# A planned order searched again, with eleven durations changed and one weight sum moved from TensorE to VectorE

## The chip, the core and the metric

The kernel runs on one core of a Trainium2 chip. The metric is the device time of one execution in microseconds (us). Before the change it is 673.11 us, the median of three runs (671.66 to 673.67). The engines are named as the profile names them: PE is TensorE's matmul and PEld its weight load, DVE is VectorE, ACT is ScalarE, POOL is GpSimd, SP is the engine that issues most DMAs.

## What is computed

An attention block with a state that is updated token by token, and then a gated feed-forward network:

```
k_n = k / (norm(k) + 1e-6)
for t in range(S):
    y[:, :, t] = einsum('bhd,bhde->bhe', q[:, :, t], state)
    v_old = einsum('bhde,bhd->bhe', state, k_n[:, :, t])
    state += beta_t * einsum('bhd,bhe->bhde', k_n[:, :, t], v_t - v_old)
x = y as (tokens, heads * 48);  xn = x / sqrt(mean(x * x) + 1e-6) * rms_g
out = (silu(xn @ w_gate) * (xn @ w_val)) @ w_out
```

There are 4 batches, 8 heads, 768 tokens and 48 elements per head, so x has 3072 rows of 384. The weights w_gate and w_val are 384 x 1536 and w_out is 1536 x 384. Weights come as 64-bit floats and are brought to 32 bits on the chip; all products are in float32.

## The kernel before

**Stages.** The tokens are cut into twelve chunks of 64 tokens for all batches and heads (c = 0 to 11). Within a chunk the recurrence is solved as a triangular system: products of k with k (`scores`, L704), an inverse built by columns on VectorE (`prep16` for c = 0 and 1, `invert` for the others, L1070 and L1076), then products with the state (L1199, L1210), with the inverse (L1281) and with q (L1317), and the new state (L1404). The result goes through the root mean square (L1445 the square on ScalarE, L1452 and L1455 the sum and the power on GpSimd, L1465 the scaling, L1475 or L1495 the product with rms_g) into the tile xf. Chunks 0 and 1 take the feed-forward part as plain products (`ffn_plain`, L1558 up and L1540 down). From chunk 2 on `ffn` makes 30 block products per chunk out of sums of weight blocks (L1651, with the sums on VectorE, L1661), and `down` seven more (L1708).

**Weights.** `weights(n0, n1)` brings 18 tiles of 128 x 768. Each is loaded as pairs of 32-bit words. ScalarE makes one part of the float from the upper word (L619), VectorE makes another from both (L607, L610, L615), and the two are added. For tile n < NPE the addition is made on TensorE, as two products with the identity into one PSUM bank (L631, L632), and ScalarE copies the bank to w_in (L636). For the other tiles one VectorE instruction adds them (L639). NPE is 1, so only tile 0 goes over TensorE; it is split in two, one of 512 and one of 256 columns.

**What sets the order.** The program has no order of its own: `P.add(engine, duration, function, priority, reads, writes, ...)` only records an operation with its duration in us, and `Plan.run` (L303) decides in what order each engine gets them. Every DMA on SP's queue is such an operation too. `forward` plays the operations through on five engines and picks, at each step, the one that could start first. It counts TensorE's instructions and lets them come in blocks of 256 (L27 and L28, `supply`): a block is asked for at one place of the block before it and lacked at a later one, and a late block lengthens the operation. Where TensorE stood still for more than 1.4 us before an operation starts, from 70 us on, 1.6 us are added for a slow clock. `backward` gives new keys from the end, `shake` moves the keys at random from a number of the list MOVES. `run` goes through the rounds and then the moves, and keeps the order with the smallest reckoned end. Until 70 us, where TensorE has nothing to do, products with the identity (L1826) are put in between to keep it running.

ScalarE's durations are written as A(n) = 0.2 + 0.0008 n, VectorE's as V(n) = 0.13 + 0.0011 n. The planner lets two neighbours of ScalarE overlap by 0.1 us.

**Lines that the change touches:** L26 ROUNDS and MOVES; L403 NPE; in `setup`, L511 the identity on GpSimd, L534 `places2` on VectorE, L535 the warm-up activation; in `weights`, L619; in `invert`, L1039 `start` (its copy is L1028) and L1040 `start2` (its copies are L1034); in `recur`, L1445, L1457 `root` (L1452 to L1455), L1465, L1475 and L1495.

## Time and profile before

| | us |
|---|---|
| median of three runs | 673.11 (671.66 to 673.67) |
| the profiled execution, its own time | 677.52 |
| its span, first to last instruction | 675.8 |
| TensorE matmul busy in the span | 657.2 |
| TensorE weight load busy | 607.2 |
| VectorE busy | 576.2 |
| ScalarE busy | 297.9 |
| GpSimd busy | 88.0 |

The profile is one execution. A line such as L1651 is a line of the kernel; where an operation is written in a helper or in a function that is handed to `P.add`, the line is that of the instruction in the function. In a list of groups, the columns after the bar are the time that the group is busy, the mean of one instruction in ns, and how long the engine stood idle just before such instructions, with what ended the wait. "issue" as a cause means that the engine waited for nothing that the profile shows. The granted clock is that of TensorE, as a share of its full speed; over the whole span it is 0.995.

### The profile page before, as it was taken

To read this page: it belongs to the slowest core of one execution; us is meant where nothing else is said; L and a number is where in the kernel's file an instruction comes from. 1 tells how busy PE (TensorE), PEld (TensorE's weight loads), DVE (VectorE), ACT (ScalarE), POOL (GpSimd) and SP (SyncE) were. 2 spreads that over 40 slices of the span, in tenths; PEclk is the share of its full clock that TensorE was granted. 3 is DMA by queue.
4 is the path that set the end of the run, shared out by engine and by line. 5 is a ranking of instruction groups with operands and counts; after the bars stand their busy time and mean duration, and the time that the engine had idled before them with its cause. 6 is when DMAs were issued, how large, how long until landed. Compare 5 with 4: busy or idle time off the path is not lost.

```text
span 675.8 us, 23477 instructions
## 1 busy us (share of the span) xinstructions
PE 657.2 (97%) x10052; PEld 607.2 (90%) x10052; DVE 576.2 (85%) x1200; ACT 297.9 (44%) x683; POOL 88.0 (13%) x105
## 2 busy tenths in 40 slices
PE   8898999999999999999899999999999999999997
PEld 6876777778799999999899999999999999999997
DVE  5998889999999998997899899899899699457473
ACT  7553543524336445345246336246345344343341
POOL 4113111031031030030030021030031001000000
PEclk9998999999999999999899999999999999999999
DMA  9574577636415457347447437457437434202100
GB/s 227 127 191 129 118 191 165 137 59 112 63 24 96 68 132 117 59 110 116 74 101 126 77 90 132 82 117 123 80 77 125 80 58 82 47 2 48 24 1 24
DMA packets 270430, 64.40 MB, mean 95 GB/s; under 512 B 256979, under 2 KB 262134, under 8 KB 270326
## 3 DMA queue, kind: packets, MB, share of 16 engines
q1 hardware_dynamic: 267046, 62.12, 46.5%
q8 instruction: 79, 1.29, 0.8%
q10 hardware_dynamic: 3280, 0.79, 0.6%
q14 instruction: 25, 0.20, 0.1%
HBM read 45.30 MB, written 17.56 MB: 93 GB/s over the span
## 4 chain that ended last, share of the span: by engine, by line
PE 65%; DVE 21%; SPq 5%; DMA 4%; issue 3%; ACT 1%; POOL 0%; DVEq 0%; POOLq 0%; ACTq 0%
PE bank L1651 35%; PE bank L1708 15%; SPq L487 5%; DVE acc L1076 4%; DVE acc L1070 3%; PE bank L1558 3%; PE bank L704 3%; PE bank L1199 2%; PE bank L1317 1%; DVE tmp L1661 1%; DMA at<-dkk 1%; PE bank L1540 1%; DVE more L1616 1%; DMA q<-in_q_dram 1%; DMA x2bd<-dx 1%
## 5 line engine op out<-in xcount | busy, mean ns | idle before, releaser
L1651 PE MATMUL bank<-xf,w_in 128*128 128x128 f32 x1440 | 179.2, 276 | 0.6 <-DVE tmp L1661 0.6
L1651 PEld LDWEIGHTS bank<-xf,w_in 128*128 128x128 f32 x1440 | 169.8, 192 | 1.7 <-DVE tmp L1661 0.8
L1661 DVE TENSOR_TENSOR tmp<-tmp,bank 128x512 f32<-128x512 f32 x180 | 119.8, 680 | 27.9 <-PE bank L1651 24.3
L1651 PE MATMUL bank<-xf,more 128*128 128x128 f32 x960 | 124.9, 277 | 1.8 <-DVE tmp L1661 1.8
L1651 PEld LDWEIGHTS bank<-xf,more 128*128 128x128 f32 x960 | 115.2, 192 | 4.3 <-DVE tmp L1661 3.2
L1663 ACT COPY tmp<-bank 128x512 f32<-128x512 f32 x120 | 68.1, 585 | 64.8 <-PE bank L1651 52.9
L1667 ACT ACTIVATE tmp<-tmp 128x256 f32<-128x256 f32 x120 | 49.7, 417 | 98.0 <-DVE tmp L1661 97.3
L731 POOL TENSOR_TENSOR knrm<-ksum,half 128x16 f32<-128x16 f32 x12 | 35.8, 2981 | 324.8 <-DVE ksum L730 309.5
L1076 DVE TENSOR_REDUCE acc<-acc 128x30 f32<-128x90 f32 (+4 forms) x150 | 70.9, 473 | 5.1
L1708 PE MATMUL bank<-wo_sb,hf 128*128 128x192 f32 x360 | 64.0, 328 | 0.0
L1708 PEld LDWEIGHTS bank<-wo_sb,hf 128*128 128x128 f32 x360 | 58.2, 191 | 0.7 <-ACT tmp L1713 0.2
L1070 DVE TENSOR_TENSOR acc<-acc,at 128x60 f32<-128x60 f32 (+4 forms) x150 | 52.7, 351 | 2.3
L1668 DVE TENSOR_TENSOR hf<-tmp 128x256 f32<-128x256 f32 x120 | 48.5, 420 | 6.6 <-ACT tmp L1667 5.5
L1540 PE MATMUL bank<-wo_sb,hf 128*128 128x384 f32 x96 | 35.3, 496 | 1.9 <-DVE hf L1566 1.8
L1558 PE MATMUL bank<-xf,w_in 128*128 128x256 f32 x144 | 34.8, 392 | 0.2 <-DVE hf L1566 0.2
L1558 PE MATMUL bank<-xp,w_in 128*128 128x256 f32 x144 | 33.8, 382 | 0.0
L1558 PEld LDWEIGHTS bank<-xp,w_in 128*128 128x128 f32 x144 | 26.8, 190 | 5.5 <-DVE hf L1566 0.3
L1558 PEld LDWEIGHTS bank<-xf,w_in 128*128 128x128 f32 x144 | 26.9, 192 | 4.7 <-DVE hf L1566 0.5
L1565 ACT ACTIVATE tmp<-bank 128x256 f32<-128x256 f32 x24 | 9.2, 383 | 43.7 <-PE bank L1558 36.4
L1713 ACT COPY tmp<-bank 128x192 f32<-128x192 f32 x30 | 9.5, 317 | 42.0 <-PE bank L1708 40.2
L1540 PEld LDWEIGHTS bank<-wo_sb,hf 128*128 128x128 f32 x96 | 17.3, 190 | 11.8 <-DVE hf L1566 3.7
L1510 DVE TENSOR_TENSOR xf<-xf 128x256 f32<-128x256 f32 (+1 forms) x70 | 24.0, 382 | 1.9 <-ACT xf L1475 1.1
(203 smaller groups left out, 988.6 us busy)
## 6 DMA issues: line engine op xcount, KB each, us to landing
at<-dkk SPq DMA_DIRECT2D x20, 256.0 KB, 3.8
more<-in_moe_w_gate_dram SPq DMA_DIRECT2D x6, 768.0 KB, 5.3
vt<-in_v_dram SPq DMA_DIRECT2D x24, 192.0 KB, 4.2
k<-in_k_dram SPq DMA_DIRECT2D x23, 192.0 KB, 4.3
out_dram<-tmp SPq DMA_DIRECT2D x46, 96.0 KB, 2.2
more<-in_moe_w_val_dram SPq DMA_DIRECT2D x5, 768.0 KB, 7.0
more<-in_moe_w_out_dram SPq DMA_DIRECT2D x5, 768.0 KB, 7.3
dsq<-k SPq DMA_DIRECT2D x6, 512.0 KB, 2.6
```

The source lines that it names most:

```text
L487: op = P.add(eng, dur + (0.08 if eng == "SP" else 0.0), lambda: queue.dma_start(out=dst, in_=src), prio, r, w, lat=0.7)
L731: P.add("POOL", 2.95, lambda: nc.gpsimd.tensor_tensor(out=knrm[i2], in0=ksum[i2], in1=half, op=ALU.pow), pn, r=[("ksum", i2), "half"], w=[ ...
L1070: nc.vector.tensor_tensor(out=acc[:, 1:3, 0:n, j + 2 : W].rearrange("p a i t -> p i a t"), in0=acc[:, old, 0:n, j : j + 2, None].to_broadc ...
L1076: nc.vector.tensor_reduce(out=acc[:, new, 0:n, j + 2 : W], in_=acc[:, lo : lo + 3, 0:n, j + 2 : W].rearrange("p a i t -> p i t a"), axis=A ...
L1540: nc.tensor.matmul(po[p].t[:, 0:DM], hf[:, spot(f), 128 * p : 128 * p + 128], wo_sb[:, spot(f)], start=(f == f0), stop=(f == f1 - 1), skip ...
L1558: nc.tensor.matmul(ps.t[:, TOK * side : TOK * side + TOK], w_in[:, side, h_, 3 * t + i_, n : n + 128], x_[:, 2 * t : 2 * t + 2].rearrange( ...
L1651: nc.tensor.matmul(g.t[:, 128 * z : 128 * z + 128], fac[:, side, 128 * f : 128 * f + 128], xf[:, xs], start=(begin and z == 0), stop=False ...
L1661: P.add("DVE", V(512), lambda t=t, g=g: nc.vector.tensor_tensor(out=t, in0=t, in1=g.t, op=ALU.add), -1, r=[g], w=[tk], last=g)
L1663: P.add("ACT", A(512), lambda t=t, g=g: nc.scalar.copy(t, g.t), -1, r=[g], w=[tk], last=g)
L1667: P.add("ACT", A(256), lambda t=t: nc.scalar.activation(out=t[:, 0:256], in_=t[:, 0:256], func=ACTF.Silu), -1, w=[tk])
L1668: P.add("DVE", V(256), lambda t=t, f0=f0, p=p: nc.vector.tensor_tensor(out=hf[:, spot(f0) : spot(f0) + 2, 128 * p : 128 * p + 128], in0=t[ ...
L1708: nc.tensor.matmul(g.t[:, 0:192], a_[:, f], b_[:, f], start=(begin and f == 0), stop=(f == 5), skip_group_check=True)
```

## The change

Three things are changed. The seeds and the numbers of moves of the search are others: 24 as seed and 20 rounds with 585 moves, where it was 22, 17 rounds and 278 moves. NPE goes from 1 to 0, so the sum of weight tile 0 is made on VectorE by the same instruction as for the other 17. And eleven durations that the planner reckons with are others. No instruction is changed otherwise, but the order of the instructions on every engine, and of the DMAs in their queues, comes out of the search anew.

```diff
-ROUNDS, MOVES = (22, 17), (22002180, 22002182, 22003335,
...
+ROUNDS, MOVES = (24, 20), (24000254, 24000519, 24001431,
...
-    NPE, NRAW, NCV = 1, 3, 2
+    NPE, NRAW, NCV = 0, 3, 2
...
-        P.add("POOL", 1.0, lambda: make_identity(nc, ident), 0, w=["ident"])
+        P.add("POOL", 0.6, lambda: make_identity(nc, ident), 0, w=["ident"])
...
-        P.add("DVE", 0.9, places2, 2, r=["ident"], w=["put"])
-        P.add("ACT", 1.7, lambda: nc.scalar.activation(out=rs[0], in_=mhalf, func=ACTF.Silu), -1, r=["half"], w=[("rs", 0)])
+        P.add("DVE", 1.32, places2, 2, r=["ident"], w=["put"])
+        P.add("ACT", 0.25, lambda: nc.scalar.activation(out=rs[0], in_=mhalf, func=ACTF.Silu), -1, r=["half"], w=[("rs", 0)])
...
-            P.add("ACT", 0.84, lambda high=high, top=top: nc.scalar.activation(
+            P.add("ACT", 0.92, lambda high=high, top=top: nc.scalar.activation(
...
-        P.add("ACT", 0.5, start, pd, r=["half"], w=AK)
-        P.add("ACT", 0.9, start2, pd + 0.5, r=bkeys, w=AK)
+        P.add("ACT", 1.05, start, pd, r=["half"], w=AK)
+        P.add("ACT", 0.66, start2, pd + 0.5, r=bkeys, w=AK)
...
-                    P.add("ACT", A(384) + 0.2, lambda p=p, gy=gy: nc.scalar.activation(
+                    P.add("ACT", A(384), lambda p=p, gy=gy: nc.scalar.activation(
...
-            P.add("POOL", 1.1 if c else 0.7, root, py, r=["half"],
+            P.add("POOL", 1.1, root, py, r=["half"],
...
-                    P.add("ACT", A(384), lambda p=p: nc.scalar.mul(yn[:, p], yn[:, p], rs[i2][:, p : p + 1]),
+                    P.add("ACT", A(384) + 0.1, lambda p=p: nc.scalar.mul(yn[:, p], yn[:, p], rs[i2][:, p : p + 1]),
...
-                    P.add("ACT", A(256), lambda k_=k_: nc.scalar.mul(xf[:, 2 * k_ : 2 * k_ + 2],
+                    P.add("ACT", A(256) + 0.09, lambda k_=k_: nc.scalar.mul(xf[:, 2 * k_ : 2 * k_ + 2],
...
-                    P.add("ACT", A(128), lambda p=p, psx=psx, k_=k_: nc.scalar.mul(
+                    P.add("ACT", A(128) + 0.07, lambda p=p, psx=psx, k_=k_: nc.scalar.mul(
```

More of the change, by code (lines that the diff above doesn't have):

```diff
@@ L25 @@
 OVERLAP = {"PE": 0.0, "ACT": 0.1, "DVE": 0.08, "POOL": 0.06, "SP": 0.0}
-ROUNDS, MOVES = (22, 17), (22002180, 22002182, 22003335, 22003342, 22003359, 22003366, 22003748, 22003755, 22003872, 22003889, 22003903, 22003920, 22003934, 22003951, 22003980, 22004653, 22004660, 22004729, 22004746, 22004753, 22004770, 22004784, 22004801, 22004870, 22004877, 22004894, 22004901, 22004918, 22004925, 22004932, 22004949, 22004994, 22005011, 22005221, 22008697, 22008780, 22010194, 22010220, 22010239, 22010256, 22010270, 22010287, 22010301, 22010318, 22010400, 22010466, 22010535, 22010559, 22010560, 22010566, 22010583, 22010590, 22010614, 22010676, 22010683, 22010700, 22010707, 22010714, 22010731, 22010738, 22013940, 22014280, 22014565, 22014620, 22014780, 22014860, 22015546, 22015640, 22016400, 22016640, 22019860, 22020512, 22020620, 22020980, 22021900, 22022178, 22022500, 22023240, 22023744, 22024759, 22025599, 22028580, 22432695, 22434395, 22436663, 22437300, 22438400, 22439440, 22441380, 22441780, 22442460, 22442900, 22730144, 22731520, 22731920, 22731968, 22731982, 22732667, 22734384, 22734484, 22734852, 22735265, 22735300, 22735678, 22736628, 22736790, 22736838, 22737523, 22737533, 22737829, 22738662, 22738951, 22740560, 22746034, 22747420, 22747741, 22748419, 22749152, 22749290, 22753826, 22754194, 22755471, 22755620, 22756220, 22756789, 22757140, 22758049, 22758160, 22759790, 22760680, 22762300, 22763820, 22766102, 22766200, 22767004, 22767644, 22767940, 22768119, 22769086, 22771213, 22773629, 22773808, 22776028, 22785537, 22851960, 22853134, 22856837, 22860912, 22861215, 22862065, 22863655, 22864481, 22865240, 22865320, 22866860, 22869820, 22898160, 22899809, 22901540, 22901620, 22902120, 22902927, 22906589, 22906700, 22907300, 22907540, 22908258, 22910819, 22910877, 22911445, 22912860, 22913386, 22918927, 22919082, 22919880, 22920476, 22922892, 22922909, 22923180, 22923960, 22924706, 22926702, 22926967, 22928120, 22928416, 22928557, 22929276, 22929700, 22938627, 22940028, 22940145, 22940630, 22942998, 22943731, 22944000, 22944137, 22944285, 22944574, 22944715, 22945414, 22946570, 22947417, 22947699, 22948384, 22948477, 22950700, 22951100, 22952944, 22955921, 22956334, 22957415, 22967671, 22968620, 23135508, 23135773, 23136045, 23136069, 23136100, 23136186, 23137876, 23138585, 23139731, 23139865, 23140612, 23140877, 23142006, 23142520, 23143245, 23144220, 23144460, 23144640, 23145389, 23146680, 23149200, 23149620, 23149700, 23149932, 23151911, 23153000, 23153329, 23155077, 23155490, 23157118, 23160928, 23161513, 23163940, 23166040, 23172120, 23180693, 23181278, 23181371, 23181691, 23181722, 23182283, 23182383, 23182407, 23182782, 23182803, 23183216, 23183388, 23183512, 23183653, 23183694, 23183949, 23184090, 23184107, 23186217, 23186499, 23186967, 23187091, 23188237, 23188502, 23191307, 23191751, 23194752, 23194814, 23196170, 23233009)
@@ new lines @@
+ROUNDS, MOVES = (24, 20), (24000254, 24000519, 24001431, 24001703, 24001720, 24001796, 24001813, 24001844, 24002412, 24002429, 24002436, 24002505, 24002529, 24002620, 24002646, 24002825, 24003699, 24004205, 24179060, 24179074, 24179098, 24179105, 24179112, 24179129, 24179140, 24179198, 24179215, 24179222, 24179277, 24179322, 24179339, 24179340, 24179353, 24179363, 24179370, 24179377, 24179401, 24179425, 24179494, 24179511, 24179525, 24179532, 24179542, 24179611, 24179618, 24179635, 24179649, 24179659, 24597779, 24597780, 24597810, 24597827, 24597903, 24597917, 24598364, 24598371, 24598395, 24598440, 24598457, 24598460, 24598471, 24598481, 24598488, 24598502, 24598620, 24598700, 24601260, 24601293, 24601307, 24601310, 24601324, 24601331, 24601334, 24601338, 24601341, 24601348, 24601355, 24601372, 24601417, 24601434, 24601441, 24601455, 24601458, 24601472, 24601482, 24601489, 24601500, 24601513, 24601520, 24601565, 24601582, 24601589, 24601600, 24601603, 24601606, 24601620, 24601630, 24601637, 24601661, 24601706, 24601723, 24601730, 24601737, 24601744, 24601751, 24601754, 24601785, 24601792, 24601861, 24601871, 24601878, 24601885, 24601895, 24601902, 24601920, 24601940, 24602002, 24602009, 24602016, 24602019, 24602026, 24602033, 24602040, 24602043, 24602050, 24602057, 24602064, 24602074, 24603280, 24603289, 24603568, 24603575, 24606056, 24606080, 24609002, 24609009, 24631655, 24631662, 24631703, 24631748, 24645394, 24645400, 24684840, 24690920, 24701668, 24701675, 24701833, 24701840, 24701909, 24701919, 24701926, 24701933, 24701940, 24701943, 24701957, 24701974, 24702050, 24702057, 24702067, 24702074, 24702098, 24702105, 24702174, 24702191, 24702205, 24702208, 24702222, 24702229, 24702236, 24702239, 24702253, 24702270, 24702340, 24702463, 24702480, 24702494, 24702501, 24702511, 24702518, 24702587, 24702600, 24702604, 24702611, 24702621, 24702628, 24702635, 24702649, 24702652, 24702659, 24702666, 24702673, 24702683, 24702690, 24702759, 24702769, 24702790, 24703805, 24704366, 24704373, 24704390, 24704442, 24704459, 24704466, 24704480, 24704483, 24704490, 24704507, 24704514, 24704520, 24704521, 24704538, 24704583, 24704590, 24704600, 24704607, 24704621, 24704628, 24704631, 24704638, 24704652, 24704655, 24704686, 24704731, 24704738, 24732520, 24732522, 24751692, 24751778, 24817117, 24817124, 24817138, 24817145, 24817148, 24817155, 24817162, 24817172, 24817179, 24817248, 24817255, 24817265, 24817272, 24817279, 24817286, 24817293, 24817296, 24817303, 24817320, 24817372, 24817389, 24817396, 24817403, 24817410, 24817413, 24817420, 24817427, 24817434, 24817437, 24817444, 24817585, 24817592, 24817616, 24817661, 24817668, 24817678, 24817692, 24817699, 24817709, 24817716, 24817733, 24817747, 24817764, 24817800, 24817809, 24817816, 24817833, 24817840, 24817847, 24817850, 24817854, 24817880, 24817888, 24817957, 24817964, 24817971, 24817974, 24817981, 24817995, 24817998, 24818005, 24818019, 24818029, 24818036, 24818081, 24818098, 24818105, 24818112, 24818115, 24818119, 24818122, 24818129, 24818143, 24818146, 24818160, 24818177, 24818246, 24818253, 24818260, 24818263, 24821006, 24822097, 24849680, 24849682, 24858637, 24869300, 24875980, 24881500, 24883780, 24885640, 24885880, 24885891, 24886607, 24888727, 24889540, 24890280, 24891040, 24892117, 24892420, 24892936, 24893848, 24894082, 24894526, 24896140, 24900780, 24901158, 24901430, 24902460, 24902841, 24902896, 24903464, 24903640, 24904321, 24904555, 24905467, 24905553, 24905732, 24906606, 24907280, 24909920, 24911562, 24911834, 24912860, 24912918, 24914515, 24916222, 24917929, 24918160, 24918208, 24920049, 24921054, 24921326, 24921500, 24923305, 24923570, 24927125, 24927156, 24929493, 24934440, 24942024, 24942857, 24944688, 24951180, 24951780, 24952077, 24952094, 24952607, 24953137, 24956052, 24956180, 24956699, 24957540, 24958000, 24958131, 24958609, 24959721, 24959817, 24959848, 24960399, 24962815, 24963245, 24965124, 24966222, 24966511, 24967623, 24967960, 24968490, 24969213, 24969330, 24970290, 24970476, 24970906, 24970980, 24972479, 24977115, 24982501, 24983093, 24985220, 24987044, 24987488, 24989680, 24989725, 24991322, 24994416, 25013985, 25018490, 25019223, 25019643, 25025122, 25026733, 25030257, 25030446, 25030800, 25030976, 25032115, 25032931, 25215798, 25216211, 25216507, 25216748, 25217302, 25308605, 25309440, 25310164, 25310422, 25310873, 25311286, 25312301, 25312480, 25315237, 25318255, 25318899, 25319064, 25319081, 25319346, 25323655, 25324220, 25332100, 25333700, 25336820, 25339540, 25339700, 25339745, 25340175, 25342894, 25347740, 25348445, 25349020, 25353240, 25355440, 25360047, 25362587, 25362980, 25363571, 25365247, 25376180, 25382445, 25400159, 25401640, 25505975, 25506147, 25506450, 25506856, 25507152, 25507689, 25692363, 25692487, 25692494, 25692520, 25692597, 25692728, 25693189, 25693306, 25777354, 25777360, 25777791, 25777932, 25861550, 25862121, 25862658, 25862806, 25862923, 25863226, 25864100, 25864348, 25864379, 25864785, 25866072, 25866516, 25867366, 25867779, 25869039, 25869056, 25869338, 25869486, 25869634, 25869782, 25869868, 25869930, 25871286, 25871754, 25871954, 25873427, 25873840, 25874855, 25874955, 25875547, 25875564, 25875736, 25876032, 25878534, 25878565, 25878713, 25878830, 25879126, 25879398, 25879508, 25879959, 25880675, 25881105, 25881549, 25881649, 25881797, 25881931, 25881962, 25882258, 25882616, 25883180, 25883239, 25883786, 26020539, 26020556, 26020773, 26021895, 26022370, 26023953, 26024187, 26024201, 26024507, 26026214, 26026937, 26027219, 26027367, 26027584, 26027632, 26029043, 26029752, 26030280, 26030764, 26031177, 26032736, 26032853, 26033982, 26034278, 26034443, 26034839, 26035689, 26035780, 26035837, 26036298, 26036422, 26037220, 26037513, 26038660, 26039072, 26041880, 26043660, 26044740, 26046200, 26047460, 26047986, 26050260, 26050581, 26051228, 26053040, 26057079, 26057600)
@@ L615, in s5 @@
                 nc.vector.scalar_tensor_tensor(out=cc, in0=low, scalar=by, in1=cc, op0=ALU.mult, op1=ALU.mult)
-            P.add("ACT", 0.84, lambda high=high, top=top: nc.scalar.activation(out=top, in_=high.bitcast(FP32), func=ACTF.Prelu, scale=2.0**-112, alpha=2.0**32), pr, r=rk, w=cak)
+            P.add("ACT", 0.92, lambda high=high, top=top: nc.scalar.activation(out=top, in_=high.bitcast(FP32), func=ACTF.Prelu, scale=2.0**-112, alpha=2.0**32), pr, r=rk, w=cak)
             P.add("DVE", 0.57, s2, pr, w=cak)
@@ L1455, in root @@
                 nc.gpsimd.tensor_tensor(out=rs[i2][:, cols], in0=ms[i2][:, cols, 0], in1=mhalf[:, cols], op=ALU.pow)
-            P.add("POOL", 1.1 if c else 0.7, root, py, r=["half"], w=[(k_, i2, p) for p in h for k_ in ("ms", "rs")])
+            P.add("POOL", 1.1, root, py, r=["half"], w=[(k_, i2, p) for p in h for k_ in ("ms", "rs")])
             if c == 0:
@@ L1464, in recur @@
                 for p in range(2):
-                    P.add("ACT", A(384), lambda p=p: nc.scalar.mul(yn[:, p], yn[:, p], rs[i2][:, p : p + 1]), py, r=[("rs", i2, p)], w=[("yn", p)])
+                    P.add("ACT", A(384) + 0.1, lambda p=p: nc.scalar.mul(yn[:, p], yn[:, p], rs[i2][:, p : p + 1]), py, r=[("rs", i2, p)], w=[("yn", p)])
             if c >= XSQ:
@@ L1474, in recur @@
                 for k_ in range(KT):
-                    P.add("ACT", A(256), lambda k_=k_: nc.scalar.mul(xf[:, 2 * k_ : 2 * k_ + 2], xf[:, 2 * k_ : 2 * k_ + 2], g_sb[:, k_ : k_ + 1]), pxv, r=["g"], w=[xkeys[0]] + ([xkeys[1]] if k_ == KT - 1 else []))
+                    P.add("ACT", A(256) + 0.09, lambda k_=k_: nc.scalar.mul(xf[:, 2 * k_ : 2 * k_ + 2], xf[:, 2 * k_ : 2 * k_ + 2], g_sb[:, k_ : k_ + 1]), pxv, r=["g"], w=[xkeys[0]] + ([xkeys[1]] if k_ == KT - 1 else []))
                 continue
```

## The prediction, on record before the result

> **What bounds the kernel.** I read the head of the page first, then the busy time by stretch, then TensorE's waits, then the order of time around the two longest of them.

> ```profile
> span 675.8 us, 23477 instructions
> ...
> PE 657.2 (97%) x10052; PEld 607.2 (90%) x10052; DVE 576.2 (85%) x1200; ACT 297.9 (44%) x683; POOL 88.0 (13%) x105
> ...
> q8 instruction: 79, 1.29, 0.8%
> ```

> TensorE (PE) is busy 97% of the span, ScalarE (ACT) 44%, GpSimd (POOL) 13%. The last line is the queue that brings instructions. TensorE has 10052 matmul and 10052 weight-load records, and 20104 over 79 is 254: so I read q8 as TensorE's own supply, one packet of 16 KB for each 256 or so of its instructions. The next lines are the busy time of TensorE (matmul, then weight load), VectorE, ScalarE and GpSimd, the granted clock and the DMA share in four stretches:

> ```profile
> 0.00:41.00 41.00, 36.21 (x816) 29.60 (x817) 32.67 (x95) 26.59 (x52) 12.22 (x23) 1.00 0.79 189
> 41.00:190.00 149.00, 143.52 (x2080) 113.57 (x2078) 138.77 (x271) 61.16 (x134) 23.83 (x19) 0.99 0.56 122
> 190.00:640.00 450.00, 445.54 (x6912) 432.40 (x6913) 386.21 (x802) 200.80 (x477) 51.93 (x64) 1.00 0.46 85
> ```

> The first product of the feed-forward part (L1558) starts at 41.02 us. Of the 36.21 us before it, 8.93 are the warming products of L1826, so that stretch is a chain of dependences. From 41 us TensorE is idle 5.5 us of 149, then 4.5 of 450. So the end is: the start of L1558, plus TensorE's own work, which a new order doesn't shorten, plus TensorE's stalls. The longest of these, from 41 us on (us in total, times, longest):

> ```profile
> PE bank L704 <- issue: 3.0, 1, 3.0
> PE bank L1651 <- DVE tmp L1661: 2.4, 6, 0.8
> PE bank L1540 <- DVE hf L1566: 1.8, 3, 0.7
> PE bank L1199 <- issue: 1.5, 1, 1.5
> PE bank L1152 <- ACT tmp L1713: 0.5, 1, 0.5
> ```

> "issue" means that no engine or transfer released the product. The order of time shows both such stalls inside runs of small products, and the windows after them show the clock (column before the DMA share):

> ```profile
> 50.28 0.99 PE L704 MATMUL bank<-qt,kt 64*64 64x64 f32 x54
> 54.28 0.34 PE L704 MATMUL bank<-qt,kt 64*64 64x64 f32 x8 [3.02 <-issue]
> ```

> ```profile
> 328.47 0.87 PE L1199 MATMUL bank<-state,qt 48*64 48x48 f32 x47
> 330.88 0.49 PE L1199 MATMUL bank<-state,qt 48*64 48x48 f32 x17 [1.54 <-issue]
> ```

> ```profile
> 55.15:58.56 3.41, 3.41 (x69) 2.58 (x67) 0.91 (x2) 0.50 (x4) 1.62 (x1) 0.50 0.51 129
> 331.63:335.04 3.41, 3.41 (x13) 3.41 (x12) 1.18 (x4) 0.64 (x2) 0.00 (x0) 0.50 0.18 26
> ```

> The one block of 64 L704 products stands still after 56, the one of L1199 after 47. In the trace a packet of q8 starts at 51.78 and takes 1.11 us, and TensorE goes on 2.5 us after its start; another starts at 328.47, and TensorE goes on 2.4 us later. So the supply came late: 64 small products pass in about 1.1 us, faster than a packet is asked for and used. After each stall the clock is half for 3.41 us, which costs 1.7 more. **Price of the two:** 3.02 + 1.54 + 2 x 1.7 = 8.0 us.

> [...]

> **The change, part by part.**

> *The first weight tile* (NPE 1 to 0). What goes: eight products on TensorE (L631, L632), in two pairs at 33.99 to 35.05 and 36.58 to 38.40, that is 2.9 us of its queue, and two copies on ScalarE (L636), 0.37 and 0.59. What comes: one sum on VectorE as in L639, 17 of which take 953 ns. The second pair stands before the transposes L1485 (38.40), but the second of these waits for L1460, which ends at 38.59 after the square root on GpSimd; without the pair, the first half of L1485 and its L1489 can go about 1.5 us earlier, and the second L1489, now at 40.21 behind a weight step of 0.55 on VectorE, about 0.8 earlier. Against this, VectorE is busy 29 to 41 us nearly without a gap, so the new 0.95 may fall on the same chain. Ends -0.8 and +0.95; I take -0.5, as the sum is due only when L1558 starts and can be put ahead of the last steps. TensorE has 16 instructions fewer, so each later packet border moves by 16 of 256 even where the order is the same.

> *The durations.* Ten of the eleven go to what the rows show: for example L1028 from 0.5 to 1.05 (1041 ns), L1034 from 0.9 to 0.66 (four of 217 less overlap), L619 from 0.84 to 0.92 (908 to 932). The eleventh goes away from it:

> ```profile
> L1445 ACT ACTIVATE bank<-yn 128x384 f32<-128x384 f32 x22 | 10.8, 489 | 12.7 <-DVE yn L1439 12.7
> L1445 ACT ACTIVATION_READ_ACCUMULATOR bank<-yn 128x1 f32 x22 | 4.1, 188 | 0.0
> ```

> The square and its read of the sum hold ScalarE 0.49 + 0.19, less some 0.10 of overlap as at L1429 (34.10 to 34.33), 0.58 us; the planner had 0.71 less 0.1 for overlap, and now has 0.51 less 0.1, so it plans 0.17 too little. These change no instruction; they only let the planner see ScalarE rightly or wrongly. ScalarE is idle 56% of the time, and it ends 0.5 us of TensorE's own waits from 41 us on. Ends: -1 (all waits on it gone, its weight-load waits counted) and +3.7 (22 squares x 0.17, all on the path). I take 0, since 22 late squares are spread over 11 chunks whose products are ready from the chunk before. The warm-up activation (1.7 to 0.25) keeps its table load of 1283 ns, ending at 5.28 just ahead of L728 at 5.42; at worst 1.3 us there, of which the chain behind has about 1 to spare.

> *The order.* All instructions are placed anew: DMAs on SP's queue, every wait, and where TensorE's packet borders fall. The planner keeps the best of 605 orders by its own reckoning, where it kept one of 295; that is no time of the chip. It does reckon with late packets, but adds the 1.6 us of a slow clock only for a gap before an operation starts, not for one inside it, and both stalls above are inside. So such stalls are undervalued before and after, and can come again. I take half of the 8.0: **-4.0**; bounds -8.0 (both gone) and +4.7 (a third, as dear as the first: 3.02 + 1.7). The other waits since 41 us, some 5 us and mostly VectorE's L1661 and L1566, I leave as they are: VectorE does the same work plus 0.95.

> **The sum.** -0.5 + 0 - 4.0 = -4.5 us against the profiled execution, whose own time is 677.52 (span 675.8 and 1.7 around it): 673.0. The median shown, 673.11, is 4.4 below that execution, about the price of the first stall. If the timed runs have both stalls, the median goes to 673.1 - 4.5 = 668.6; if they lack the first, only the second's 3.2 is left to halve: 673.1 - 0.5 - 1.6 = 671.0. Between the two I forecast **670.0**.

> **Rivals.**
> 1. *The stalls only move* (0.17). The 79 packets stay, each asked for somewhere; two again fall into small products. Only the -0.5 is left: 672.6. For it: six tenths of TensorE's products are small ones (L704 1536, L1199 1344, L1317 768, L1404 704, L1281 640 and smaller groups, of 10052). Against: two of 79 borders stall over 1 us now, so orders can avoid them.
> 2. *The issue stalls are not supply* (0.05), but something that a new order keeps: also 672.6. [...] The packets beside both stalls speak against it.
> 3. *A third border in small products* (0.22), the slower side. Place: a run of 64-row products such as L956 with L704, or the two states of L1199. Price 4.7, so 677.8. It decides from three issue stalls over 1 us in the trace instead of two; with fewer it can't be this.
> 4. *The short square* (0.06). L1452 and the chain to xf come late, TensorE waits at a chunk's first L1651. Half of 3.7 plus the 0.95 of VectorE: 675.9.

> **The numbers.** Forecast 0.50. Its own range is 664.6 (673.1 less 0.5 and all of the 8.0) to 671.0. The range of 8 in 10 reaches from 664.5, just past that, to 678, past rival 3. A measurement of this kernel can tell about 0.3%, 2.0 us, from no change. Faster than 671.1: 0.50; within: 0.22 (rivals 1 and 2); slower than 675.1: 0.28 (rivals 3 and 4).

> **What would show it.** TensorE's waits on issue from 41 us on: one over 1 us instead of two, and one window of half clock. L1558 first at about 40.5. No L631, L632 and L636, and 18 sums at L639. TensorE's busy sum lower by 2 to 3 us, VectorE's about 1 higher. q8 still 79 packets. Wrong, if the issue stalls are fewer and the time is the same, or if waits on VectorE's L1661 or L1566 take their place, which I left at 5 us.

## The result, and the profile after

The changed kernel takes 676.66 us (median of 20 runs, 672.24 to 678.37), the kernel before 672.72 us beside it (median of 20 runs, 669.62 to 675.33). The ratio is 1.0052, with a 95% interval of 1.0037 to 1.0067: the change makes the kernel slower, by 3.9 us between the medians and by 3.5 us by the ratio, where 670.0 was forecast. The recorded profile of the changed kernel points the other way:

```profile
span 670.5 us, 23483 instructions
...
PE 652.7 (97%) x10050; PEld 603.4 (90%) x10050; DVE 578.1 (86%) x1201; ACT 296.7 (44%) x681; POOL 88.5 (13%) x105
...
q8 instruction: 79, 1.29, 0.8%
```

Its span is 5.3 us shorter than that of the profile before, and TensorE's waits from 41 us on show even less than the one wait on issue over 1 us that had been forecast (us in total, times, longest):

```profile
PE bank L1651 <- DVE tmp L1661: 2.2, 3, 1.0
PE bank L1540 <- DVE wo_sb L639: 1.3, 1, 1.3
PE bank L1558 <- issue: 1.0, 1, 1.0
PE bank L1199 <- issue: 0.7, 1, 0.7
PE bank L1540 <- issue: 0.6, 1, 0.6
```

No wait on issue is over 1.0 us, and the granted clock is 1.00 over the whole span. But this execution took 672.24 us, the shortest of the twenty, while the profile before was of one with 677.52, longer than any of its twenty timed runs. Neither is a typical execution. So both kernels were profiled again, unedited.

### The profile page after: what moved, and what is told of

Its sections match the earlier page's. It is cut to its first block, busy times and chain, and to the rows that moved or that the text cites. A ratio compares the mean times of both kernels' runs of the same rounds, so it can differ in the third digit from the quotient of the medians.

```text
span 670.5 us, 23483 instructions
## 1 busy us (share of the span) xinstructions
PE 652.7 (97%) x10050; PEld 603.4 (90%) x10050; DVE 578.1 (86%) x1201; ACT 296.7 (44%) x681; POOL 88.5 (13%) x105
## 3 DMA queue, kind: packets, MB, share of 16 engines
q8 instruction: 79, 1.29, 0.8%
## 4 chain that ended last, share of the span: by engine, by line
PE 73%; DVE 16%; DMA 5%; issue 2%; SPq 2%; ACT 1%; POOL 1%; ACTq 0%; DVEq 0%; POOLq 0%
PE bank L1651 36%; PE bank L1708 21%; DVE acc L1076 3%; PE bank L1199 3%; PE bank L704 2%; DVE acc L1070 2%; PE bank L1317 2%; PE bank L1558 2%; DMA dxt<-acc 2%; SPq L487 2%; PE bank L1307 1%; DVE tmp L1661 1%; PE bank L1281 1%; DMA q<-in_q_dram 1%; PE bank L1404 1%
## 5 line engine op out<-in xcount | busy, mean ns | idle before, releaser
L1651 PE MATMUL bank<-xf,w_in 128*128 128x128 f32 x1440 | 178.3, 276 | 0.0
L1651 PEld LDWEIGHTS bank<-xf,w_in 128*128 128x128 f32 x1440 | 169.9, 192 | 1.0 <-DVE tmp L1661 0.4
L1661 DVE TENSOR_TENSOR tmp<-tmp,bank 128x512 f32<-128x512 f32 x180 | 119.5, 681 | 32.7 <-PE bank L1651 28.0
L1651 PE MATMUL bank<-xf,more 128*128 128x128 f32 x960 | 126.3, 278 | 2.3 <-DVE tmp L1661 2.2
L1651 PEld LDWEIGHTS bank<-xf,more 128*128 128x128 f32 x960 | 115.3, 192 | 5.1 <-DVE tmp L1661 3.6
L1540 PE MATMUL bank<-wo_sb,hf 128*128 128x384 f32 x96 | 34.5, 495 | 2.0 <-DVE wo_sb L639 1.3
L1558 PE MATMUL bank<-xf,w_in 128*128 128x256 f32 x144 | 34.5, 386 | 1.0 <-issue 1.0
L1558 PE MATMUL bank<-xp,w_in 128*128 128x256 f32 x144 | 33.5, 382 | 0.0
L1558 PEld LDWEIGHTS bank<-xf,w_in 128*128 128x128 f32 x144 | 26.4, 190 | 5.9 <-issue 1.6
L1558 PEld LDWEIGHTS bank<-xp,w_in 128*128 128x128 f32 x144 | 26.8, 190 | 4.4
L1540 PEld LDWEIGHTS bank<-wo_sb,hf 128*128 128x128 f32 x96 | 17.5, 190 | 12.8 <-DVE wo_sb L639 1.7
L1096 POOL COPY acc<-acc 128x128 f32<-128x128 f32 x40 | 18.4, 491 | 48.6 <-DVE acc L1076 47.9
L1713 ACT COPY tmp<-bank 128x192 f32<-128x192 f32 x30 | 9.6, 319 | 33.8 <-PE bank L1708 32.6
```

Source lines behind the costliest of these rows:

```text
L1540: nc.tensor.matmul(po[p].t[:, 0:DM], hf[:, spot(f), 128 * p : 128 * p + 128], wo_sb[:, spot(f)], start=(f == f0), stop=(f == f1 - 1), skip ...
L1558: nc.tensor.matmul(ps.t[:, TOK * side : TOK * side + TOK], w_in[:, side, h_, 3 * t + i_, n : n + 128], x_[:, 2 * t : 2 * t + 2].rearrange( ...
L1651: nc.tensor.matmul(g.t[:, 128 * z : 128 * z + 128], fac[:, side, 128 * f : 128 * f + 128], xf[:, xs], start=(begin and z == 0), stop=False ...
L1661: P.add("DVE", V(512), lambda t=t, g=g: nc.vector.tensor_tensor(out=t, in0=t, in1=g.t, op=ALU.add), -1, r=[g], w=[tk], last=g)
```

## First experiments: both kernels again, and the packet borders moved

> The changed kernel once more, unedited, for a second profile and more times. Its one profiled execution took 672.24 us, 4.4 below its median of 676.66, with a granted clock of 1.0, while most of its timed executions show 0.995 to 0.997. Theory A (a late packet of TensorE's instructions in most executions, which the recorded profile happened not to have): the median is again 676 to 677, and an execution near it has at least one wait on issue over 1 us from 41 us on that the recorded profile lacks, followed by a window of half clock. Theory B (waits that the new order brings on VectorE and ScalarE): the issue waits stay under 1 us, and an execution near the median has 4 us more of waits on L1661, L1566, L639.

> The kernel before once more, unedited. Its recorded profile took 677.52 us, 4.8 above its median of 672.72. Theory A: the median is again 672 to 673.5, and a profile near it lacks one of the two issue stalls (3.0 at L704 and 1.5 at L1199) with its half clock. Theory B: both stalls stay, and other waits are shorter.

The repeat of the changed kernel has a median of 676.18 us (ratio 1.0038, 1.0016 to 1.0061), and its profiled execution is near it: 675.99. The repeat of the kernel before has 672.68 (1.0002, 0.9983 to 1.0022), its profiled execution 672.09. These two profiles are compared here. First the order of time on TensorE in the repeat of the changed kernel:

```profile
34.84 0.25 PE L1404 MATMUL bank<-u,k 64*48 64x48 f32 x2
37.09 1.53 PE L1404 MATMUL bank<-u,k 64*48 64x48 f32 x62 [2.00 <-issue]
38.55 2.93 PE L1826 MATMUL bank<-ident 128*128 128x512 f32 x4
41.27 2.47 PE L1485 MATMUL bank<-xp,yn 128*128 128x128 f32 x12
43.58 0.82 PE L1826 MATMUL bank<-ident 128*128 128x256 f32 x4
44.48 1.53 PE L1558 MATMUL bank<-xf,w_in 128*128 128x256 f32 x6
```

and the same place in the recorded profile of the changed kernel:

```profile
36.95 0.93 PE L1404 MATMUL bank<-u,k 64*48 64x48 f32 x62 [1.45 <-issue]
37.81 1.56 PE L1826 MATMUL bank<-ident 128*128 128x512 f32 x4
39.20 1.50 PE L1485 MATMUL bank<-xp,yn 128*128 128x128 f32 x12
40.54 0.82 PE L1826 MATMUL bank<-ident 128*128 128x256 f32 x4
41.45 1.53 PE L1558 MATMUL bank<-xf,w_in 128*128 128x256 f32 x6
```

After two products of L1404 TensorE stands still with nothing to release it: in the trace of the repeat a packet of its instructions starts at 34.35, and TensorE goes on 2.7 us after that; in the recorded profile one starts at 34.21, and TensorE goes on at 36.95, also 2.7 us later. In the repeat the wait is 2.00 instead of 1.45 us, and then the same two warming products take 2.93 instead of 1.56, and the transposes L1485 2.47 instead of 1.50. The clock tells why (the column before the last two):

```profile
36.47:43.30 6.83, 6.21 (x76) 4.90 (x76) 3.61 (x11) 2.83 (x7) 1.32 (x3) 0.50 0.41 117
```

It is half for 6.83 us, in the stretch that the feed-forward part waits for. L1558 starts at 44.48 instead of 41.45. So theory A had the right kind of stall, a late packet and half clock, but looked for it from 41 us on, and it lies at 35 us. Of the 4 us more that theory B expected on VectorE's lines there is no sign against the recorded profile.

The same place in the repeat of the kernel before:

```profile
35.94 0.31 PE L1317 MATMUL bank<-u,pt 64*64 64x48 f32 x2 [0.51 <-issue]
36.19 1.12 PE L631 MATMUL bank<-xf,ident 128*128 128x512 f32 x2
37.15 1.02 PE L632 MATMUL bank<-tmp,ident 128*128 128x512 f32 x2
38.01 1.50 PE L1485 MATMUL bank<-xp,yn 128*128 128x128 f32 x12
39.44 0.94 PE L1404 MATMUL bank<-u,k 64*48 64x48 f32 x64
40.30 0.49 PE L1826 MATMUL bank<-ident 128*128 128x128 f32 x2
40.63 4.05 PE L1558 MATMUL bank<-xf,w_in 128*128 128x256 f32 x18
```

From the first L1558 to the end the repeat of the changed kernel needs 674.3 - 44.5 = 629.8 us, and that of the kernel before 670.4 - 40.6 = 629.8 us. **In this pair of profiles the whole difference is the start of L1558.**

The repeat of the kernel before also corrects what was read from its first profile:

```profile
PE bank L1199 <- issue: 1.5, 1, 1.5
PE bank L1651 <- DVE tmp L1661: 1.5, 4, 0.8
PE bank L1540 <- DVE hf L1566: 1.4, 3, 0.6
PE bank L704 <- issue: 1.0, 1, 1.0
```

The stall at L1199 is there again, with its half clock (0.996 over this execution); that at L704 is 1.0 us and not 3.0, and the clock from 41 to 190 us is 1.00, where it was 0.99 in the first profile:

```profile
326.83 0.49 PE L1199 MATMUL bank<-state,qt 48*64 48x48 f32 x17 [1.48 <-issue]
```

So the equal 629.8 us hide two differences that cancel. The time of the kernel before holds this stall and its half clock, 1.48 + 1.7 = 3.2 us; the new order has 0.3 us of issue waits at L1199 and full clock there: the 6.83 us at half clock before it, 3.4 of 674.3, account for all of its 0.995. It spends as much elsewhere from 41 us on: TensorE's waits on the weight sum L639 (1.3 us) and on issue at L1558 (1.0) and L1540 (0.6) are new, and the rest is not traced. The gain that was forecast for this stall came, and was lost again elsewhere.

The half clock alone isn't the loss either. One stretch of 3.41 us at half clock brings the mean clock of an execution to 0.997, by an estimate from 1.7 of some 670 us. Of the 32 timed executions of the unedited changed kernel 7 have a clock over 0.998, with a median of 674.5 us, and 18 have 0.996 or 0.997, with 676.6. Of the 105 of the kernel before that list a clock, 47 are over 0.998, with 671.4, and 48 have 0.996 or 0.997, with 673.1. At the same clock the changed kernel is 3.1 to 3.5 us slower. Its repeat, with two stretches and 0.995, is one of only 7 with 0.995 or less, and none of its slower executions at full clock was profiled.

The next two kernels move the packet borders and nothing else: the first 41 us get six warming products more, of the same total width, so that every border comes 24 instructions earlier.

```diff
-                    filler(fillers(pe, s))
+                    cut, more_ = [], fillers(pe, s)
+                    for w_ in more_:
+                        while w_ > 1 and split:
+                            cut.append(1)
+                            w_, split = w_ - 1, split - 1
+                        cut.append(w_)
+                    filler(cut)
```

> The changed kernel with the same order, but six more warming products of the same total width in the first 41 us, so that every border of TensorE's 256-instruction packets falls 24 instructions earlier in the work. Theory A: the time moves by more than 2 us, one way or the other, from 676.6. Theory B: it stays within 1 us of 676.6.

> The kernel before with the same six more warming products, borders 24 instructions earlier. Theory A: the time moves by more than 2 us from 672.7, more likely up, since its borders lie well in most executions. Theory B: within 1 us of 672.7.

The changed kernel stays at 676.55 (1.0062, 1.0041 to 1.0083). Theory B's 1 us holds, and theory A isn't refuted by it: in the profile the border has moved out of L1404 into the end of L1317, where the wait on issue is 2.16 us at 35.25 and the clock halves at 38.64, so 24 instructions seem to have been too few to leave the dense run. The kernel before goes to 671.39 (0.998, 0.9957 to 1.0003). A second sample was taken later:

> The kernel before with the packet borders 24 instructions earlier, once more: its first median was 671.39, 0.998 of before with an interval that just reaches 1. If the borders matter there, the ratio is again 0.997 to 0.999, and most executions show a clock over 0.998, where before has 0.997 in about half; if not, 1.000 within 0.001.

It gives 671.12 (0.9986, 0.9970 to 1.0002), and 10 of 12 executions have a clock over 0.998, as in the first sample; of the unedited kernel before beside it 13 of 29. In the profiles of both samples the stall at L1199 and its half clock are gone (the clock is 0.999 over the execution of the first, and 0.997 over that of the second, with one stretch at another place). So moving the borders changes there how often the clock is half. The medians fall by 1.3 and 1.7 us, but each interval still just takes in 1.

The second sample's profile shows one more thing. At 35.4 us TensorE waits 1.84 us on issue inside L1317, the clock is half from 38.68 to 42.09, and L1558 comes at 43.74, nearly as late as in the repeat of the changed kernel, with both wide pairs in place. From there on it needs 627.6 us, 2.2 less than the repeat of the kernel before. So a late start is not peculiar to the new order, and the wide pairs don't always prevent it.

## What the standstill costs, and what hides behind it

In the following two kernels the border stays, and what TensorE has around it is changed. In the first the two warming products ahead of L1485 (widths 4 and 2; operation 140) run ahead of L1404 (operation 150); in the second they are dropped.

```diff
-                if s < until:
+                if op.n == 150:
+                    filler([4, 2])
+                elif s < until and op.n != 140:
                     filler(fillers(pe, s))
```

> The changed kernel with the two warming products that stand behind the products of L1404 (ahead of L1485) put ahead of L1404 instead; nothing else moves, and every count is the same. Theory A (the cost is TensorE's standstill of 1.5 to 2.2 us at L1404 near 35 us, where a packet of instructions is late, with the slow clock behind it): wide products pass few instructions in much time, so the packet comes while they run; no issue wait over 1 us there, full clock, first L1558 at 41 to 41.5 instead of 43.7 to 44.5, and a median of 672.5 to 673.5 instead of 676.4. Rival B (waits that the new order brings after 41 us): the first L1558 may come earlier, but the median stays at 676 within 1 us.

> The changed kernel without those two warming products. Theory A: the standstill at L1404 stays, near 2 us, but L1485 no longer queues behind warming products at half clock (2.9 us in the profile of the repeat); L1558 first at 41.5 to 42.5, median 673.5 to 675. If the standstill alone were the cost and the products behind it none, 676.4 would stay. Rival B: 676 within 1 us.

Dropped: 673.86 (1.0023, 1.0005 to 1.0042), a median as theory A expected. The wait at L1404 is 2.55 us in its profile, with 3.4 us of half clock (L1485 takes 2.93 us instead of 1.50, and the clock is 0.997 over the execution), but L1558 starts at 42.6. The time falls by 2.5 us although the standstill stays. Of the 3.9 us between 44.5 and 40.6 some 1.9 would then be the warming products themselves, at half clock ahead of L1485; this is an estimate, as it compares two executions with 6.83 and 3.41 us of half clock.

Put first: 674.91 (1.0027, 1.0005 to 1.0049), a gain of only 1.5 us where 3 to 4 were expected, which lies between theory A and rival B. The start did what it should: the wait on issue is 0.64 us at 36.3, the clock is 0.999 over the execution, L1558 starts at 41.2. But the end came no sooner in proportion, and the profile names the place (TensorE, then VectorE; lines of this edited kernel are two higher, so L1201 is L1199, L1025 L1023 and L1524 L1522):

```profile
89.14 1.49 PE L1201 MATMUL bank<-state,kt 48*64 48x48 f32 x64 [2.10 <-DVE state L1524]
```

```profile
85.00 1.23 DVE L1025 TENSOR_TENSOR at<-at,beta_b 128x1024 f32<-128x1024 f32 x1 [2.97 <-DMA q<-in_q_dram]
86.26 1.13 DVE L1050 TENSOR_TENSOR acc<-at 128x512 f32<-128x512 f32 x1
...
88.60 0.95 DVE L1524 TENSOR_TENSOR state<-state,bank 128x384 f32<-128x384 f32 x2
```

TensorE waits 2.1 us for the new state. The state's sum stands behind L1025 on VectorE, and that had itself waited for a DMA. The trace's releaser is the last transfer to land, here a load of q; on SP's queue the second half of at<-dkk, which L1025 reads, stood behind seven loads of q from 73.68 to 80.95. In the kernel before there are six loads there, and they took 3.1 us. The new order brought this wait, but it isn't there in every execution: in the recorded profile of the changed kernel, with L1558 at 41.45, the same seven loads took 5.6 us instead of 7.2, and TensorE doesn't wait there. In the repeat, with L1558 at 44.48, it doesn't either.

Two kernels test that. One moves only this DMA, to stand behind the first half of at<-dkk; the other does so in the kernel with the warming products first.

```diff
-            op.fn()
+            if op.n != 350:
+                op.fn()
+            if op.n == 349:
+                next(o for o, _ in best[1] if o.n == 350).fn()
```

> The changed kernel with one DMA moved: the second half of at<-dkk for chunk 2 is issued right behind the first, ahead of the loads of q that stand between them in SP's queue. If the start before 41 us sets the time of the changed kernel, TensorE isn't late for what hangs on that DMA (L1023, then the state's sum L1522), and the median stays at 675.5 to 676.7. If the DMA's place is a cost of its own, 674 to 675.

> Both at once: the warming products ahead of L1404 (after_warm_first, 674.91) and the DMA moved. In after_warm_first the first L1558 came 3 us earlier, but TensorE then waited 2.1 us at 87 us for the state's sum, which stood behind L1023 on VectorE and so behind that DMA. If this is where the gain went, the wait is under 0.5 us and the median is 672.5 to 673.5; if not, 674.9 within 1 us.

The DMA alone: 676.22 (1.0067, 1.0044 to 1.0091), nothing gained. Both: 673.20 (1.0025, 1.0010 to 1.0041), and the wait at 87 us is gone from the profile; TensorE's longest there from 41 us on is now 1.3 us, on the weight sum L639. By the medians, warming products and DMA give 1.5 and 0 us alone and 3.0 together. But the ratios with and without the moved DMA, 1.0025 (1.0010 to 1.0041) and 1.0027 (1.0005 to 1.0049), lie within each other: that the DMA's place gains time is shown by the profile and not by the times. What the times do show is that the start matters. With only the warming products dropped or put first, the ratio falls from 1.0052 and 1.0038 in the unedited changed kernel to 1.0023 and 1.0027, so about half of the loss goes. By the medians 0.7 us is left with both edits, by the ratio 1.7, and this is not traced further.

## The weight tile's sum

The first kernel takes the order before and makes the sum of tile 0 on VectorE, in the place of L631's first pair; both pairs and their copies go. The second also puts warming products of the same widths and number in the places of the pairs.

```diff
+HOOK, SKIP = {}, {37, 38, 39, 40}
...
+            for fn in HOOK.get(op.n, ()):
+                fn()
...
-            op.fn()
+            if op.n not in SKIP:
+                op.fn()
...
+                    HOOK[39] = [lambda dst=dst, top=tiled(top_), cc=tiled(cc_): nc.vector.tensor_tensor(out=dst, in0=top, in1=cc, op=ALU.add), lambda: filler([2, 2])]
+                    HOOK[37] = [lambda: filler([4, 4])]
```

(`filler` in the second kernel only.)

> The kernel before, in its own order, with the first weight tile's sum on VectorE alone: the pairs of L631 and L632 and their copies go, one sum of 0.95 us on VectorE comes in the place of the first. Theory A: without the pairs the halves of L1317 run on, the packet is late by 1.5 us or more there, the clock halves, and L1558 comes 1 to 3 us later than 40.6; median 674 to 676 instead of 672.7. The step as the prediction priced it (-0.5): 672.2.

> The kernel before with the first weight tile's sum on VectorE, as in before_tile0_dve (673.96, 1.0025 of before), but with warming products of the same widths and number in the places of L631 and L632. If what the pairs did was to keep TensorE running until L1460 lets L1485 go (in before_tile0_dve TensorE stood 1.6 us at 35.6 and its clock was half from 39.5), the clock stays full, L1558 comes at 40.6 to 41 and the median is 672 to 673. If the sum's 0.95 us on VectorE is the cost, 674 stays.

The sum on VectorE costs: 673.96 (1.0025, 1.0005 to 1.0045), just under the 674 to 676 that theory A gave. Its mechanism was another than expected there. The packet isn't late; TensorE has nothing to do (lines are five to six higher; L1322 is L1317, L1490 L1485, L1465 L1460):

```profile
34.15 1.45 PE L1322 MATMUL bank<-u,pt 64*64 64x48 f32 x62
37.22 0.94 PE L1490 MATMUL bank<-xp,yn 128*128 128x128 f32 x6 [1.62 <-DVE xp L1465]
38.96 1.14 PE L1490 MATMUL bank<-xp,yn 128*128 128x128 f32 x6 [0.81 <-DVE xp L1465]
40.03 1.53 PE L1409 MATMUL bank<-u,k 64*48 64x48 f32 x64
```

TensorE waits for the factors that the transposes need, and then its clock is half from 39.48 to 42.89, so that L1409, 0.94 us in the repeat of the kernel before, takes 1.53; L1558 starts at 42.1. With warming products in the same places it is 672.69 (1.0002, 0.9988 to 1.0017), and L1558 starts at 41.2. None of the twelve executions without them has a clock over 0.998, and six of the twelve with them do. So the 0.95 us on VectorE cost nothing that can be measured; what cost 1.5 us was the loss of wide products that kept TensorE running.

The last kernel puts the pairs back into the changed order. It changes the computation: its pairs come after the third tile's words are in the first tile's buffers, so another sum goes into tile 0; shapes and counts are as they would be.

> The changed kernel with the first weight tile's sum back on TensorE, two pairs of wide products: one between the two halves of L1317, one ahead of L1404, with their copies on ScalarE behind L1429; the sum on VectorE goes. Order and durations are otherwise those of the change. Theory A, which puts the loss on the cover that these pairs gave: no issue wait over 1 us at 35 us, L1558 first near 41, median 672 to 673.5. Rival B: 676 within 1 us, so that the sum's place doesn't matter.

It takes 677.32 us (1.0080, 1.0049 to 1.0111), against theory A's 672 to 673.5 and rival B's 675 to 677. In its profile the wait on issue at 36.2 is down to 0.96 us, so the cover works, but pairs and warming products together now stand ahead of L1485, which starts at 41.56, and L1558 at 43.7. A later wait on issue of 1.93 us at 78.5, with half clock (0.997 over the execution), is in that profile too. So this run doesn't show that the missing pairs are what made the changed kernel slower. Wide products helped here where TensorE would have been idle (1.5 us in the order before), and not where more of them stood ahead of L1485.

## Why the prediction was wrong, step by step

**What bounds the kernel.** Right: the start of L1558, then TensorE's own work, then stalls. But the start was taken over nearly unchanged, at about 40.5 us, and only stalls from 41 us on were priced.

**The price of the two stalls, 8.0 us.** Taken from one execution 4.8 us above the median. The one at L704 is 3.0 us there and 1.0 in the repeat, so its 4.7 was mostly not there to win. The prediction saw that the difference of profile and median was about this stall's price, and still let it count for about half: 670.0 lies between 668.6 with it and 671.0 without.

**The first weight tile, -0.5.** This failed in sign: +1.5 us in the order before (ratio 1.0005 to 1.0045). The two pairs were priced as work in the way of L1485. They stood in a gap in which L1485 waits for L1460 anyway; that was in the same paragraph of the working (38.59 against 38.40), but half clock behind a wait, 3.41 us of it here when the pairs were gone, was reckoned only for stalls after 41 us.

**The durations, 0.** No run takes them alone, since they act only through the order. Left open. The count of ten that go to the rows is one too many: the warm-up activation takes 1283 ns of table load and 205 ns of its own, 1.49 us, which is nearer to 1.7 than to 0.25.

**The order, -4.0.** This is the step that failed most, in two places. First, it had no term for a stall that the new order brings before 41 us. In the repeat L1558 starts at 44.48 us instead of 40.6: L1317 and L1404 stand back to back, with no wide product between them, the packet is late in L1404 (2.00 us), and the clock is half for 6.83 us. In the order before, the wide pairs interrupt L1317, and L1404 comes after the transposes; the wait on issue was 0.51 us in the repeat. Edits at this place alone take back 1.5 and 2.5 us. Second, it left the other waits after 41 us as they were. The stall at L1199 did go, worth 3.2 us, but the repeats need the same 629.8 us from L1558 on, so as much was lost there again, 1.3 us of it on L639 and 1.6 on issue at L1558 and L1540.

**Rival 3** had the mechanism, a further border in small products, and a time of 677.8 against 676.66 measured. It had 0.22, and named two wrong places. That its time is so near is partly luck: it added a third stall to two that stay, where the stall at L1199 went and other waits came. Its test, three stalls from 41 us on instead of two, would have missed the one that mattered. Rivals 1 and 2 gave 672.6; the border moved by 24 instructions speaks against rival 2. Rival 4, the short square, wasn't needed: no wait of TensorE on that chain stands out.

**What stays open:** the part of the loss that is left when the start is mended (0.7 us by the medians, 1.7 by the ratio), why the changed kernel is 3.1 us slower in executions at full clock too, and whether the kernel before with its borders moved (0.998 and 0.9986) is really faster; no edit here is faster than the kernel before beyond its interval.

## What to carry to other kernels

Before a stall in one profile is priced, compare that execution's own time with the median; where it lies 0.7% off, the stall may be what is off. Where two kernels need the same time in some stretch, look whether the same things make it up; here a stall that had gone hid waits that had come. Ask of every wide product that a change takes away what TensorE would do in its place: where it stood idle instead, that cost 1.5 us here. And where a gain at the start should show at the end, look how far the DMAs and the other engines' queues have come by then; here TensorE waited 2.1 us of it at 87 us in one profile, for a DMA behind seven loads.

## What the runs showed of the hardware

Of TensorE's waits on issue of 0.6 us or more in the two recorded profiles all but one (0.62 us at L1540 in the profile after) end at steps of 256 in its stream: behind 1473, 1985 and 10433 of its instructions in the profile before (L1317, L704, L1199), and behind 1473, 3009 and 10433 in the profile after (L1404, L1558, L1199). The differences are 512, 1536, 7424 and 8448, multiples of 256. Each of the 79 packets of q8 has 16384 bytes there.
